# Moving the gain row's product and the second queries' transposes in the opening of a fused attention and feed-forward kernel

## The chip, the cores and the metric

The kernel runs on one core of one Trainium2 chip. The metric is the device time of one execution in microseconds (us), lower is better. A time "of the runs" is the median of several executions; durations of single instructions come from one profiled execution. The engines are TensorE (PE, with PEld for its weight loads), VectorE (DVE), ScalarE (ACT), GpSimd (POOL) and SyncE (SP); a trailing q, as in SPq, is an engine's instruction queue.

## What is computed

Chunked attention with 8 memory keys per head, then a feed-forward block with layer norm and residual. Cut to what matters (B=4, H=8, S=768, D=64, so tokens have 512 features; the hidden width is 2048):

```python
for c in range(nc):                       # chunks of 32 queries
    q_c = q[:, :, c_start:c_end]
    k_full = concat([mem_k, k[:, :, l_start:r_end]])   # 16 left, 8 right
    v_full = concat([mem_v, v[:, :, l_start:r_end]])
    a = softmax(scale * q_c @ k_full.T)
    out[:, :, c_start:c_end] = a @ v_full
x = out.transpose(0, 2, 1, 3).reshape(B, S, 512)
xn = (x - mean) / sqrt(var + 1e-6) * g_ln
return x + relu(xn @ w_ch1) @ w_ch2
```

## The kernel before, in words

The 3072 tokens are 24 tiles of 128. For a tile, `scores` multiplies turned keys (`KT`) and turned queries (`QT`) on TensorE and ScalarE takes the exponentials into `AT` (line 294); `values` multiplies `AT` with `V` (line 307); `norm` divides, sums and writes `xn` = (x - mean) * `g_row` on VectorE (lines 317 to 327); `turn_x` turns `xn` into `xT`. `up` (line 375) multiplies by `w_ch1` and `down` (line 392) by `w_ch2`, three tiles to a unit, eight units. From unit 0 on, a hand-written plan puts the attention steps of the next unit between the `up` and `down` steps of this one. The schedule is manual: each engine runs its instructions in the order in which the code issues them.

The change lies in the opening, before unit 0, where nothing but the order written out in lines 455 to 551 sets what runs when:

- Line 471, `stay_busy(10)`: ten products of zeros (`busy`, 128x128 by 128x512), whose results nobody reads. `stay_busy(n, p)` writes them to the PSUM buffer `p`, or to a slot of the `mm` ring. "Zero products" below are these.
- Line 472, `clear_v` with `clear_k`: memsets on VectorE. Line 473, `mem_keys`: four small products turn the memory keys (line 167), VectorE copies them to `memKT` (line 173). Line 474, `mem_cols`: VectorE spreads them into `KT` (line 177).
- Lines 513 to 522: the first turned keys, that is the transposes (line 187) of head pairs 0 and 1 of batch 0, 32 products; two zero products; the first turned queries, 32 products; then, on VectorE, four copies into `KT` (line 202), on ScalarE two into `QT` (line 210), on VectorE `keep_mem` (line 144); three zero products.
- Lines 523 to 532: the second keys (pairs 2 and 3), four zero products, the second queries, and their copies, of pair 2 on ScalarE and of pair 3 on VectorE.
- Lines 533 and 534: `g_row`, the gain row `g_one` (1x512, fp32) repeated over 128 partitions by a product with a column of ones, into `mm` buffer `banks[2]`; VectorE copies it to SBUF.
- Lines 535 to 563: scores, values and norms of tiles 0 to 2 with more zero products between them, then the first `up` steps, which need the weights `w1c`.

The buffer `spare`, where the zero products between the transposes go, is half 0 of `att` buffer 0. Each `att` buffer has two halves of 512 floats.

GpSimd issues the loads of keys, queries, values and weights through its DMA queue, in the written order. SyncE issues `memk32`, `g_one` and `memv32` (lines 459 to 461) first, and later the stores.

The softmax here doesn't subtract the row's maximum and nothing guards it: scores larger than these inputs give would overflow.

## Time and profile before

| What | Value |
|---|---|
| Median of 8 runs | 217.43 us (215.36 to 218.54) |
| The profiled execution: its own time | 218.06 us |
| The profiled execution: span of the trace | 216.3 us |
| PE busy | 209.2 us, 97% of the span |
| PEld busy | 124.1 us, 57% |
| DVE busy | 113.5 us, 52% |
| ACT busy, POOL busy | 91.3 us, 91.5 us, 42% each |
| Granted TensorE clock, mean | 0.99 |
| The two products of line 533 | 1.12 us busy |
| The copy of line 534 | 0.69 us |
| The 35 zero products in the opening | 26 into `mm`, 9 into `att` |

The profile lists busy time by engine and by line, the chain of work that ended last (followed back from the last instruction to what released each step), a timeline with the idle time before a group in brackets and what ended it, and windows with the granted clock. Starts are microseconds from the span's start. A line `start, length, engine, line, operation, output<-inputs, shape, xcount` of the timeline is a group of equal instructions.

### The profile page before, as it was taken

The page shows a single profiled execution, that of the slowest core. Times are in us where ns is not written, and L with a number is a line of the kernel's source. Part 1 is how long each engine was busy: PE and PEld are TensorE (multiplying, and loading weights), DVE is VectorE, ACT ScalarE, POOL GpSimd, SP SyncE. Part 2 cuts the span into 40 slices and gives each one's busy share as a digit, 9 for nine tenths or more (in the row PEclk, how much of TensorE's full clock was granted, in tenths as well). Part 3 has the DMA queues.
Part 4 walks back from the last instruction along what each step waited for, and adds up shares of the span by engine and source line. Part 5 has one row for each costly group of instructions (what it writes and reads, how often), then busy time and mean ns, then how long its engine had stood idle before and what let it go on. Part 6 is the DMA issues. An engine that isn't in the chain of part 4 may idle for free.

```text
span 216.3 us, 5336 instructions
## 1 busy us (share of the span) xinstructions
PE 209.2 (97%) x2173; PEld 124.1 (57%) x2173; DVE 113.5 (52%) x268; ACT 91.3 (42%) x187; POOL 91.5 (42%) x169
## 2 busy tenths in 40 slices
PE   7989999999999999999989999999999999999994
PEld 2545876457755566546644566447644665457553
DVE  4657484585747548524365349415375438534222
ACT  4354535954573666302734077203761175303200
POOL 7992244689998228810003999520112000400000
PEclk9988999999999999999999999999999999999999
DMA  5999999999999959995305999997693201230012
GB/s 81 159 128 194 204 216 185 192 206 247 139 139 171 127 155 127 113 202 144 54 2 100 122 179 158 148 186 82 175 141 109 84 3 24 77 122 0 0 52 97
DMA packets 87611, 27.26 MB, mean 126 GB/s; under 512 B 78289, under 2 KB 84081, under 8 KB 87538
## 3 DMA queue, kind: packets, MB, share of 16 engines
q0 software_dynamic: 62128, 14.38, 75.0%
q1 hardware_dynamic: 25458, 12.54, 26.3%
q8 instruction: 17, 0.28, 0.5%
q14 instruction: 8, 0.07, 0.1%
HBM read 28.84 MB, written 6.29 MB: 162 GB/s over the span
## 4 chain that ended last, share of the span: by engine, by line
PE 86%; DMA 6%; DVE 3%; issue 1%; POOL 1%; SPq 1%; ACT 1%; POOLq 0%; DVEq 0%; ACTq 0%
PE mm L392 38%; PE mm L375 33%; DMA V<-V 4%; PE att L307 4%; PE att L287 3%; DMA kraw<-in_k_dram 2%; PE att L187 2%; PE mm L364 2%; PE mm L410 2%; PE mm L187 1%; DVE xn L327 1%; DVE xs L318 1%; PE att L350 1%; ACT AT L294 1%; PE mm L533 0%
## 5 line engine op out<-in xcount | busy, mean ns | idle before, releaser
L375 PE MATMUL mm<-xT,w1c 128*128 128x384 f16 (+2 forms) x528 | 87.9, 322 | 0.1
L392 PE MATMUL mm<-w2c,rT 128*128 128x512 f16 x368 | 84.2, 379 | 0.0
L375 PEld LDWEIGHTS <-w1c 128*128 128x128 f16 x528 | 57.9, 114 | 24.8 <-issue 0.6
L381 ACT ACTIVATE rT<-mm 128x384 f16<-128x384 f32 (+2 forms) x66 | 31.7, 484 | 76.2 <-PE mm L375 54.8
L392 PEld LDWEIGHTS <-rT 128*128 128x128 f16 x368 | 34.4, 98 | 38.4
L383 DVE TENSOR_SCALAR rT<-mm 128x384 f16<-128x384 f32 (+2 forms) x66 | 35.6, 542 | 33.7 <-PE mm L375 33.3
L399 DVE SCALAR_TENSOR_TENSOR osb<-mm,rstd,xs 128x512 f32<-128x512 f32 x23 | 17.3, 751 | 42.4 <-PE mm L392 31.1
L294 ACT ACTIVATE AT<-att,band 104x512 f16<-104x512 f32 x48 | 29.5, 688 | 11.8 <-PE att L287 11.8
L336 POOL TENSOR_SCALAR veps<-squares 128x1 f32<-128x1 f32 x24 | 5.1, 214 | 54.3 <-ACT junk L333 53.0
L116 POOL DMA_DIRECT2D V<-in_v_dram x24 | 18.4, 773 | 12.2 <-DMA w1c<-in_moe_w_ch_dram 9.0
L333 ACT ACTIVATE junk<-xs,nmean 128x512 f16<-128x512 f32 x24 | 17.4, 724 | 7.7 <-DVE nmean L324 6.9
L327 DVE SCALAR_TENSOR_TENSOR xn<-xs,nmean,g_row 128x512 f16<-128x512 f32 x24 | 18.0, 752 | 0.9
L318 DVE SCALAR_TENSOR_TENSOR xs<-att,rec 128x512 f32<-128x512 f32 x24 | 16.6, 691 | 0.8
L274 POOL COPY KT<-KT 128x128 f16<-128x128 f16 (+4 forms) x16 | 4.3, 294 | 23.9 <-DMA KT<-kraw 23.9
L340 POOL TENSOR_TENSOR rstd<-veps,mhalf 128x1 f32<-128x1 f32 x24 | 13.2, 551 | 2.0
L307 PEld LDWEIGHTS <-AT 104*64 104x64 f16 x384 | 7.7, 112 | 8.5 <-issue 3.4
L122 POOL DMA_DIRECT2D V<-in_v_dram x16 | 12.0, 798 | 0.1
L247 POOL DMA_DIRECT2D qraw<-in_q_dram x12 | 11.4, 946 | 0.0
L247 POOL DMA_DIRECT2D kraw<-in_k_dram x12 | 11.3, 942 | 0.0
L307 PE MATMUL att<-V,AT 104*64 104x65 f16 x384 | 9.7, 199 | 1.6 <-DMA V<-V 0.9
L317 DVE RECIPROCAL rec<-att 128x8 f32<-128x8 f32 x24 | 4.9, 203 | 11.7 <-ACT AT L294 6.0
L364 PE MATMUL mm<-busy 128*128 128x512 f16 x26 | 9.2, 490 | 1.2 <-DVE counts L456 1.2
(76 smaller groups left out, 118.2 us busy)
## 6 DMA issues: line engine op xcount, KB each, us to landing
out_dram<-osb SPq DMA_DIRECT2D x23, 256.0 KB, 2.4
V<-in_v_dram POOLq DMA_DIRECT2D x36, 96.0 KB, 6.2
w1c<-in_moe_w_ch_dram POOLq DMA_DIRECT2D x4, 512.0 KB, 10.9
w2c<-in_moe_w_ch_dram POOLq DMA_DIRECT2D x4, 512.0 KB, 14.5
kraw<-in_k_dram POOLq DMA_DIRECT2D x12, 128.0 KB, 5.6
qraw<-in_q_dram POOLq DMA_DIRECT2D x12, 128.0 KB, 5.7
qraw<-in_q_dram POOLq DMA_DIRECT2D x3, 384.0 KB, 12.2
kraw<-in_k_dram POOLq DMA_DIRECT2D x3, 256.0 KB, 4.9
```

The source lines that it names most:

```text
L116: nc.gpsimd.dma_start(out=V[b % 2][r : r + hi - lo, g, :, 0:64], in_=dram(v, b * H * HS + lo * D, [[64, hi - lo], [HS, H], [1, 64]]),)
L247: nc.gpsimd.dma_start(out=free(dst, 512 * t, [[64, H], [1, 64]]), in_=dram(src, b * H * HS + 128 * t * D, [[D, 128], [HS, H], [1, 64]]),)
L294: nc.scalar.activation(out=free(a, 32 * c, [[512, 2], [64, 8], [1, 32]], KR), in_=free(p, 32 * c, [[512, 2], [64, 8], [1, 32]], KR), func= ...
L307: nc.tensor.matmul(out=p[64 * gg : 64 * gg + 64, h // 4, c0 : c0 + 65], lhsT=AT[t % 3][0:KR, h % 2, 4 * gg + h // 2, :], rhs=V[b % 2][0:KR ...
L318: nc.vector.scalar_tensor_tensor(out=x.rearrange("p (h d) -> p h d", h=H), in0=free(p, 0, [[128, H], [1, 64]]), scalar=1.0, in1=free(r, 0, ...
L327: nc.vector.scalar_tensor_tensor(out=xn[i], in0=x, scalar=nmean[i], in1=g_row, op0=ALU.add, op1=ALU.mult,)
L333: nc.scalar.activation(out=junk, in_=xs[xi], func=ACTF.Square, bias=nmean[i], accum_out=squares[i],)
L375: nc.tensor.matmul(out=p, lhsT=free(w, i, [[4, 128]]), rhs=xT[u % 2][:, dt, lo:hi], start=(dt == 0), stop=(dt == 3),)
L381: nc.scalar.activation(out=o, in_=p, func=ACTF.Relu)
L383: nc.vector.tensor_scalar(out=o, in0=p, scalar1=0.0, scalar2=None, op0=ALU.max)
L392: nc.tensor.matmul(out=p, lhsT=rT[hc][:, 128 * i : 128 * i + 128], rhs=w2c[hc // 4][:, hc % 4, :], start=(hc == 0), stop=(hc == 15),)
L399: nc.vector.scalar_tensor_tensor(out=o, in0=p, scalar=rstd[t % 9], in1=xs[t % 9], op0=ALU.mult, op1=ALU.add,)
```

## The change

The product for `g_row` and its copy move from behind the second queries to the front. The product stands behind the ten zero products and ahead of `mem_keys`; its output is now half 1 of `att` buffer 0, whose half 0 is the `spare` of the zero products. The copy stands behind `mem_cols` and so ahead of the copies of the first turned keys. Behind the second keys two zero products are left of four, then come the second queries, and three zero products stand where the product for `g_row` was.

```diff
     stay_busy(10)
     clear_v(0, nc.vector, lambda: clear_k(0), 33)
+    spare = att[(turn["att"] + 2) % 2]
+    nc.tensor.matmul(out=spare[:, 1, :], lhsT=ones32, rhs=g_one, start=True, stop=True)
     mem_keys()
     mem_cols(0)
+    nc.vector.tensor_copy(out=g_row, in_=spare[:, 1, :])
     for g in range(3):
         load_v_group(0, g)
...
     stay_busy(3, spare)
     for j in range(2, 4):
         turn_kq(first_k[j], k16[0], j, CUT[0])
-    stay_busy(4, spare)
+    stay_busy(2, spare)
     for j in range(2, 4):
         turn_kq(first_q[j], q16[0], j, CUT[1])
...
     for j in range(2, 4):
         keep_q(on[j], first_q[j], 0, j, CUT[1], 0, 6)
-    nc.tensor.matmul(out=banks[2], lhsT=ones32, rhs=g_one, start=True, stop=True)
-    vec(out=g_row, in_=banks[2])
+    stay_busy(3, spare)
     scores(0, 0)
     scores(0, 1)
     stay_busy(2)
```

## The prediction, made before the changed kernel ran

> **What bounds the kernel now.** I read the page first: PE is busy 209.2 of 216.3 us, and the chain of waits gives PE 86%. So whatever delays PE in the opening delays the end, unless something later absorbs it. The change touches only the opening, so the next view is that chain in order of time (start, length, what):

> ```profile
> 3.66 4.88 DMA kraw<-in_k_dram
> 8.53 0.04 issue
> 8.58 0.69 PE mm L187 x32
> 9.27 0.97 PE att L364 x4
> 10.24 0.61 PE mm L187 x32
> 10.85 1.05 PE mm L533 x2
> 11.90 0.36 PE att L287 x16
> ```

> Up to 8.53 a load sets the pace: the second keys can't be turned before it lands. From there to the first scores PE itself is the chain: second keys, four zero products, second queries, product for `g_row`. The timeline of VectorE shows what the copies do beside it (start, length, line, shape, idle time before):

> ```profile
> 5.11 0.29 DVE L173 CAST memKT<-mm 128x128 f16<-128x128 f32 x1 [1.56 <-PE mm L167]
> 5.44 0.26 DVE L177 COPY KT<-memKT 128x384 f16<-128x384 f16 x1
> 5.96 1.60 DVE L202 COPY KT<-mm 128x72 f16<-128x72 f16 x4 [0.27 <-PE mm L187]
> ...
> 7.59 0.96 DVE L144 COPY V<-memv 8x3072 f16<-8x3072 f16 x1
> ...
> 9.31 0.85 DVE L202 COPY KT<-mm 128x72 f16<-128x72 f16 x2 [0.76 <-PE mm L187]
> ...
> 10.89 0.56 DVE L210 COPY QT<-mm 128x384 f16<-128x384 f16 x1 [0.73 <-PE mm L187]
> ```

> VectorE has about 0.8 us of slack twice. The windows (busy time of PE, PEld, DVE, ACT, POOL, then granted clock, DMA share, GB/s) show one more thing: a stretch at half clock behind the scores.

> ```profile
> 4.00:7.40 3.40, 2.95 (x75) 1.65 (x74) 1.99 (x6) 0.21 (x1) 3.36 (x8) 1.00 1.17 185
> 7.40:10.80 3.40, 3.01 (x75) 1.66 (x72) 1.97 (x4) 1.74 (x5) 3.24 (x10) 1.00 1.70 150
> 10.80:14.20 3.40, 2.75 (x57) 1.35 (x54) 1.25 (x2) 2.17 (x5) 3.40 (x5) 1.00 1.55 100
> 14.20:17.60 3.40, 3.40 (x38) 1.55 (x37) 3.17 (x10) 1.60 (x3) 2.67 (x5) 0.50 1.17 177
> ```

> Last, how far an earlier PE could get. GpSimd's timeline:

> ```profile
> 20.13 0.80 POOL L116 DMA_DIRECT2D V<-in_v_dram  x1 [3.26 <-DMA w1c<-in_moe_w_ch_dram]
> ```

> GpSimd was held until the first `w1c` landed, and PE's first weight load from `w1c` starts at 20.09. The first `up` products start at 20.50. The same view shows it held for the second, third and fourth `w1c` until 22.63, 25.18 and 28.25. So the opening can gain at most about 20.50 - 20.09 = 0.4 us; a loss passes through in full, since PE has no idle time behind it to give.

> **Part 1: the product for `g_row` ahead of the memory keys.** It costs PE the same 1.05 us, at 4.82 instead of 10.85. Its input is there: `memv32`, issued after `g_one` on SP's queue, landed by 3.60. (No other queue is passed: no DMA moves, and GpSimd's and SP's orders are the same.) So `mem_keys` starts at 4.82 + 1.05 = 5.87, and lasts 0.25 us, to 6.12. The first keys started at 5.48 when their load landed; now they start at 6.12 and, at 0.62 us (5.48 to 6.10), end at 6.74.

> **Part 2: the copy, and the wait it brings.** On VectorE `memKT` follows `mem_keys` by 5.11 - 4.82 = 0.29: 6.16. `mem_cols` starts 0.33 later, 6.49; the copy after 0.26 + 0.03, at 6.78, and lasts 0.69, to 7.47. The diff doesn't say that somebody waits for this, but the changed program as built does: the first zero product behind the first keys writes the same `att` buffer as the product for `g_row`, and waits for VectorE; the last thing VectorE was given before it is that copy. In the old program it waits for nobody. PE is free at 6.74 and gets on at about 7.52 (a release takes 0.04 to 0.06 us, as from the exponentials' end at 13.62 to the values at 13.66). Queued behind it on PE is everything: two zero products (0.97/4 = 0.243 each, 0.49), first queries (0.62), three zero products (0.73): 7.52 + 1.84 = 9.36. That takes the place of the wait for the load until 8.53, so the second keys start 9.36 - 8.58 = 0.78 us later.

> **Part 3: behind the second keys.** Two zero products fewer ahead of the second queries: -0.49. Three zero products (0.73) instead of the product (1.05): -0.32. From 9.36: keys 0.69, two zero products 0.49, queries 0.61, three zero products 0.73, so the scores are due at 11.88, against 11.90. The sum on PE is 0.78 - 0.49 - 0.32 = -0.03 us.

> **Part 4: are the copies in time?** VectorE: the four copies of line 202 start behind the new copy at 7.50 and end at 9.10, `keep_mem` 9.13 to 10.09, the copy of pair 3's keys (0.73 behind the start of their turning, 9.36) 10.12 to 10.97. Its queries are turned from 9.36 + 0.69 + 0.49 = 10.54, the copy follows by 0.65 (10.24 to 10.89): 11.19 to 11.75. ScalarE's last copy: 10.54 + 0.40 = 10.94 to 11.42. Both end before 11.88, VectorE's with 0.13 us to spare; three zero products are its cover. If that is gone, the scores of pair 3 wait for it, by what it is late. The copy of `g_row` that leaves 11.94 ran while VectorE had nothing else, so it gives nothing.

> **Part 5: the clock.** Half clock from 14.2 to 17.6 costs in the chain 1.30 us for three zero products at 14.10, and the same at 16.52, against 0.65 for three at 18.04; 16 value products take 0.58 at 15.40 against 0.37 at 18.69. Without it, the second values would wait for the exponentials (end 14.77) and start at 14.82 instead of 15.40, and after both triples `up` could start some 1.5 us earlier, but `w1c` allows 0.4. The stretch before the half clock held 2.75 us of busy PE, with the product for `g_row`, 48 small products and one idle gap of 0.65; the stretches at 4.0 and 7.4 held 2.95 and 3.01 and were not followed by half clock. The change moves that product into 4.0 to 7.4, where the new wait also puts an idle gap of 0.63 (6.74 to 7.37); 10.8 to 14.2 gets zero products instead. No row tells what the gate counts, so I bound it: neither stretch at half clock, -0.4; half clock only moved ahead, to 7.4: zero products at 0.43 (1.30/3) and transposes at 0.58/0.37 of their time put the scores 1.33 later, but then the full clock behind 14.2 gives that back, `up` at 20.26, -0.2; both stretches, `up` at 21.15, +0.65. I take "as before", 0, between them.

> The row first: half clock came after a gap of only 0.65 us. [...]

> One more bound: the ten zero products were 0.43 us apart up to 3.78 and about 0.22 from then on. Where that step comes later in an execution, the product for `g_row` and the first keys run slow as well: up to 1.05 + 0.35 = +1.4 us. The other end is the -0.4.

> **Sum.** -0.03 on PE, 0 from copies, 0 from the clock: 218.06 - 0.03 = 218.03 us for the profiled execution. That execution is 0.63 us above the median of the runs (217.43), so for the median 217.4 us: no change.

> **Rivals.**
> - *The clock gate takes the new opening worse* (slower). Place: 7.4 to 10.8, with the product for `g_row` and the 0.63 us wait in the stretch before, and 14.2 to 17.6 still at half. For it: the stretch that was punished had the same product and the same size of gap. Against: 0.86 us of zero products at its start. Price +0.65 us, with the slow opening up to +1.4: 218.1 to 218.8. It decides if both stretches are granted 0.50. Chance 0.25.
> - *The clock stays full* (faster). For it: the product leaves 10.8 to 14.2 for zero products. Price -0.4, capped by `w1c`: 217.0. Chance 0.20.
> - *The new wait doesn't bite*, for example since the copy runs earlier. Then the second keys start at 8.58 as before and PE is due at the scores at 8.58 + 2.52 = 11.10, but VectorE (four copies to 9.1, and the rest as in part 4 without a gap: 10.09, 10.95, 11.53) holds pair 3's scores until 11.58: -0.3, 217.1. Against it: the built program has the wait. Chance 0.08.
> - *No change*, as forecast, the remaining 0.47.

> **Numbers.** 1% is 2.2 us, about what a measurement of this kernel can tell from no change. No case reaches that: not the gains, because of `w1c`, and not the losses, unless several meet. The runs themselves spread from 215.36 to 218.54. For the range I put some 0.8 us of that beside the ends -0.4 and +1.0 (middle of the slow rival): 216.2 to 219.2. Faster by over 1%: 0.05, for scatter; slower by over 1%: 0.09, the slow rival with a second loss; within 1%: 0.86.

> **What would show it.** Right: the first zero product behind the first keys waits on VectorE's copy until about 7.5; second keys at about 9.4, no longer released by a load; scores at about 11.9; first `up` between 20.1 and 21.2. Wrong: second keys at 8.6 (no wait), scores held by VectorE's last copy, half clock in a stretch other than 14.2 to 17.6, or any difference behind 21 us that isn't carried over from the opening.

## The result, and the profile after

| | before | after |
|---|---|---|
| Median of the runs | 217.47 us (32 runs, 215.26 to 219.18) | 220.5 us (11 runs, 219.48 to 221.42) |
| Ratio to before | | 1.0169, 95% interval 1.0136 to 1.0202 |
| Profiled execution: time, span | 218.06, 216.3 us | 220.38, 218.7 us |
| Mean granted clock of the profiled execution | 0.99 | 0.977 |
| First scores start, first `up` starts | 11.90, 20.50 us | 15.34, 23.46 us |

The change costs 3.0 us by the medians of all runs; forecast was none, and the range ended at 219.2. Ratios and their intervals leave out executions that lie more than 1.5% above the fastest of the same kernel (so 1.0169 is more than 220.5/217.47); where this hides part of a kernel's executions, the text gives those too.

The chain of waits of the changed kernel (start, length, what), from the first zero products to the first scores:

```profile
1.24 4.42 PE mm L364 x10
5.66 1.05 PE att L474 x2
6.71 0.20 PE mm L167 x4
...
7.52 0.61 DVE g_row L477
8.13 0.04 issue
8.17 0.59 PE att L364 x2
8.77 0.85 PE att L187 x23
9.61 1.40 PE att L364 x3
11.01 0.99 PE mm L187 x17
12.00 0.97 PE att L364 x2
12.97 0.98 PE mm L187 x17
13.95 1.40 PE att L364 x3
15.34 0.96 PE att L287 x24
```

PE's timeline has the wait beside the first zero product that follows the first keys:

```profile
8.17 0.59 PE L364 MATMUL att<-busy 128*128 128x512 f16 x2 [0.66 <-DVE g_row L477]
```

So the wait for the copy is there, with the order that was foreseen. But three zero products take 1.40 us where the sum had 0.73, and the second keys 0.99 instead of 0.69. The windows say why (busy time of PE, PEld, DVE, ACT, POOL, each with its count, then granted clock, DMA share, GB/s):

```profile
5.20:8.60 3.40, 2.74 (x42) 1.20 (x40) 1.63 (x5) 0.00 (x0) 3.20 (x13) 1.00 1.23 181
...
8.80:12.00 3.20, 3.20 (x68) 1.97 (x67) 2.10 (x4) 1.24 (x4) 3.20 (x4) 0.52 2.02 132
12.00:15.40 3.40, 3.40 (x45) 1.40 (x45) 1.41 (x3) 0.82 (x2) 3.40 (x6) 0.50 1.28 117
15.40:18.70 3.30, 3.27 (x52) 1.68 (x49) 0.59 (x2) 2.42 (x4) 1.23 (x4) 0.50 1.23 200
...
18.90:19.10 0.20, 0.20 (x2) 0.00 (x0) 0.17 (x3) 0.00 (x0) 0.20 (x1) 0.50 1.30 195
19.10:19.30 0.20, 0.20 (x3) 0.06 (x4) 0.17 (x2) 0.00 (x0) 0.20 (x1) 0.86 1.16 195
```

From about 8.9 to 19.15 the clock is halved: 10.2 us, three times the 3.4 us of the one stretch in the old profile (14.2 to 17.6), while PE is busy nearly all the time. That is one execution; the mean clock stands beside every one. "A halved stretch", below, is 3.4 us of half clock, as in the old profile. Half clock over 10.2 of 218.7 us makes a mean of 1 - 10.2 x 0.5 / 218.7 = 0.977; by the same sum one stretch of 3.4 makes 0.992 and two make 0.984. Of 12 executions of the changed kernel (the eleven of the table and one of 220.11 us) 11 have 0.974 to 0.977. Of 67 of the old one, run beside the experiments, 40 have 0.997 or more (median 216.9 us), 19 have 0.990 to 0.992 (217.3), 7 have 0.983 or 0.984 (218.3), one has 0.975 (221.3). So the time goes with the number of halved stretches that the mean stands for, in the old kernel too, and the change moves nearly all executions to three. The longer start of the changed profile (its ten zero products take 4.42 us against 3.64) is not what brings the half clock: below, they take 4.45 us in a run whose opening shows none, and 3.86 us in one with four halved stretches.

At the first `up` the changed kernel is 23.46 - 20.50 = 2.96 us late, at the end 2.4. Part comes back at one place: the old kernel's values of unit 2 waited 0.9 us for the transfer `V<-V`, until 109.96; in the changed kernel no product waits for it, though one waits 0.2 us for VectorE's `rT`. So the prediction's "PE has no idle time behind it to give" was not quite right.

### The profile page after: what moved, and what is told of

Its sections match the earlier page's. It is cut to its first block, busy times and chain, and to the rows that moved or that the text cites. A ratio compares the mean times of both kernels' runs of the same rounds, so it can differ in the third digit from the quotient of the medians.

```text
span 218.7 us, 5338 instructions
## 1 busy us (share of the span) xinstructions
PE 212.8 (97%) x2174; PEld 125.6 (57%) x2174; DVE 113.4 (52%) x268; ACT 91.2 (42%) x187; POOL 91.5 (42%) x169
## 4 chain that ended last, share of the span: by engine, by line
PE 95%; DVE 3%; issue 0%; DVEq 0%
PE mm L375 37%; PE mm L392 37%; PE mm L364 4%; PE att L307 4%; PE att L287 3%; PE att L187 2%; PE att L364 2%; PE mm L410 2%; PE mm L187 2%; DVE xn L327 1%; DVE xs L318 1%; PE att L350 1%; PE att L474 0%; DVE rT L383 0%; DVE KT L177 0%
## 5 line engine op out<-in xcount | busy, mean ns | idle before, releaser
L116 POOL DMA_DIRECT2D V<-in_v_dram x24 | 18.9, 792 | 10.4 <-DMA w1c<-in_moe_w_ch_dram 7.7
L122 POOL DMA_DIRECT2D V<-in_v_dram x16 | 12.0, 796 | 0.1
L317 DVE RECIPROCAL rec<-att 128x8 f32<-128x8 f32 x24 | 4.9, 203 | 12.3 <-PE att L307 7.5
L364 PE MATMUL mm<-busy 128*128 128x512 f16 x26 | 9.9, 522 | 1.2 <-DVE counts L456 1.2
L287 PEld LDWEIGHTS <-KT 64*128 64x128 f16 x384 | 6.8, 97 | 6.0 <-issue 5.9
```

The lines of the kernel that those rows point to most:

```text
L116: nc.gpsimd.dma_start(out=V[b % 2][r : r + hi - lo, g, :, 0:64], in_=dram(v, b * H * HS + lo * D, [[64, hi - lo], [HS, H], [1, 64]]),)
L364: nc.tensor.matmul(out=p, lhsT=busy[:, 0:128], rhs=busy, start=True, stop=True)
```

## The experiments

The edits are against the changed kernel, unless said otherwise. All ratios are to the kernel before, on the same chip.

**The wait away.** The product goes where no zero product writes:

```diff
-    spare = att[(turn["att"] + 2) % 2]
-    nc.tensor.matmul(out=spare[:, 1, :], lhsT=ones32, rhs=g_one, start=True, stop=True)
+    nc.tensor.matmul(out=mm[1], lhsT=ones32, rhs=g_one, start=True, stop=True)
...
-    nc.vector.tensor_copy(out=g_row, in_=spare[:, 1, :])
+    nc.vector.tensor_copy(out=g_row, in_=mm[1])
```

> The changed kernel with the product for g_row written to buffer 1 of the mm ring, which the zero products between the transposes don't use; so no zero product waits for the copy. Theory A (the clock gate: the 3.4 us stretch that holds the product and the 0.66 us wait has too few dense products, and the gate halves the clock for three stretches; the wait is the larger part): half clock at most one stretch, mean clock 0.99, ratio to before 0.997 to 1.005, first up at about 20.5. Theory B (the product itself, one row of fp32 for 1.05 us, is what starves the gate; the wait hardly matters): half clock still from about 9, clock 0.977, ratio 1.010 to 1.017, first up at 22.8 to 23.4. Theory C (fewer zero products behind the second keys): as B.

Ratio 0.9963 (0.9921 to 1.0004). Median of all ten executions 217.08 us; three of them, at 218.63, 218.87 and 222.7, stand outside the ratio. In the profiled execution (215.79 us) the first `up` starts at 19.52, and with the product in front but no wait the clock stays at 1.00:

```profile
5.20:8.60 3.40, 3.40 (x58) 1.61 (x58) 1.29 (x5) 0.00 (x0) 3.20 (x13) 1.00 1.25 182
8.80:12.00 3.20, 3.20 (x86) 1.80 (x80) 3.14 (x7) 2.06 (x5) 3.20 (x4) 1.00 2.06 133
```

The long half clock is gone as a rule: theory A, not B or C. Two details speak for the product too: with it in front, the clock record still has two halved stretches in two of ten, and the execution of 222.7 us, with a recorded clock of 1.0, is of the kind that the last section describes.

**The front alone.** Rear as before, product and copy in front:

```diff
-    stay_busy(2, spare)
+    stay_busy(4, spare)
     for j in range(2, 4):
         turn_kq(first_q[j], q16[0], j, CUT[1])
...
-    stay_busy(3, spare)
     scores(0, 0)
```

> Only the front of the change: product and copy ahead of the memory keys and first keys; behind the second keys four zero products as before, and nothing where the product was (so five zero products fewer on that path than four plus the product, by time). Theories A and B: half clock from about 9 as in the changed kernel, clock 0.977, ratio 1.012 to 1.02. Theory C (the two zero products that are missing behind the second keys): no long half clock, ratio below 1.005. A sum of path lengths alone would give 9.36 + 0.69 + 0.97 + 0.61 = 11.63 for the scores, 0.27 us earlier than before.

Ratio 1.018 (1.0105 to 1.0255), clock 0.967 in the profiled execution, half clock from 7.8 to 21.5, four stretches:

```profile
8.00:21.40 13.40, 13.11 (x192) 6.68 (x191) 6.52 (x16) 5.12 (x11) 9.48 (x15) 0.50 1.42 159
```

The front does the harm without the rear; theory C falls.

**The rear alone** (against the kernel before):

```diff
-    stay_busy(4, spare)
+    stay_busy(2, spare)
...
     vec(out=g_row, in_=banks[2])
+    stay_busy(3, spare)
```

> Only the rear of the change: two zero products instead of four behind the second keys, the product for g_row and its copy where they were, and the three zero products behind them. Theories A and B: no half clock before 14, at most one stretch, clock 0.99 or more; by path the scores come 0.73 - 0.49 = 0.24 us later, ratio 1.000 to 1.003. Theory C: half clock from 9 to 12 on, ratio above 1.01.

Ratio 0.9983 (0.9948 to 1.0017); one of ten executions had clock 0.974 and 221.81 us, the others lie from 216.17 to 217.51. The profiled one has a single halved stretch, but from 11.1 and for 3.4 us, not behind 14 as expected: it again follows the stretch with the product for `g_row`, which runs from 10.1 to 11.1 here. The rear costs nothing that could be measured.

**Zero products in place of the product, the wait kept:**

```diff
-    nc.tensor.matmul(out=spare[:, 1, :], lhsT=ones32, rhs=g_one, start=True, stop=True)
+    stay_busy(5, spare[:, 1, :])
```

> The changed kernel with five zero products (5 x 0.216 = 1.08 us) in place of the product for g_row, into the same half of the same buffer; the copy and the wait for it stay. g_row is then all zeros, so the layer norm's output, and with it the feed-forward part, is left at zero; the instructions and their order are otherwise the same. Theory A: the wait is still there, so still half clock for part of the opening, ratio 1.006 to 1.017. Theory B: the gate has its dense products, clock 0.99 or more, ratio 0.997 to 1.005 in spite of the wait.

Ratio 0.9973 (0.9938 to 1.0007), all ten executions from 215.76 to 217.87, clock never under 0.997. This is the run that breaks theory A as stated, for the wait is there in full. The timeline of PE (line numbers one higher than in the changed kernel):

```profile
5.21 1.24 PE L365 MATMUL att<-busy 128*128 128x512 f16 x5
6.38 0.25 PE L168 MATMUL mm<-identity,memk 128*64 128x64 f16 x4
6.56 0.69 PE L188 MATMUL mm<-identity,kraw 64*64 64x64 f16 x32
7.91 0.59 PE L365 MATMUL att<-busy 128*128 128x512 f16 x2 [0.66 <-DVE g_row L478]
```

The idle time is the same 0.66 us, to the hundredth, as in the changed kernel, and so is the busy time of PE from 5.2 to 8.6:

```profile
5.20:8.60 3.40, 2.74 (x54) 1.47 (x54) 1.89 (x6) 0.00 (x0) 3.18 (x13) 1.00 1.22 177
8.80:12.00 3.20, 3.20 (x92) 1.91 (x86) 2.69 (x5) 2.06 (x5) 3.20 (x4) 1.00 1.91 128
```

**The wait covered.** Three more zero products that wait for nothing, ahead of the two that do:

```diff
+    stay_busy(3, first[:, 0, :])
     stay_busy(2, spare)
     for j in range(2):
         turn_kq(first_q[j], q16[0], j, CUT[1])
```

> The changed kernel with three zero products more, into a buffer that nothing holds (half 0 of att buffer 1), ahead of the two that wait for the copy: the 0.66 us wait is filled, the wait itself and the order of all else stay. Theory D (what decides is how much dense product the 3.4 us stretch holds; product for g_row and idle time are both thin, and either may be replaced): no run of half clock over three stretches, mean clock mostly 0.99 to 1.0, ratio 0.996 to 1.005. Theory E (the wait delays the copies, and this, not the idle time of TensorE, is what the changed kernel pays for): still 1.010 to 1.017.

Ratio 0.9997 (0.9954 to 1.0041). Eight of ten executions from 215.77 to 217.96, and two at 221.75 and 222.63, outside the ratio, of which below. Theory D; E would have needed 1.010 or more. Work was added to PE, and the ratio went from 1.0169 to 0.9997. The execution that was profiled is the one of 222.63 us, so that the filled wait is shown by the times and the recorded clocks of the eight (0.997 or more), not by a trace.

**More zero products where the clock is already halved:**

```diff
     keep_mem(0, 0, 6, vec)
-    stay_busy(3, spare)
+    stay_busy(6, spare)
```

> The changed kernel with six zero products instead of three behind the first queries, where the clock is already halved. Theory D (a stretch at half clock ends when the next one holds enough dense product, and the transposes count for little): the first halved stretch has 6 x 0.43 = 2.6 us of dense product and is the last or last but one, mean clock 0.984 to 0.992 in place of 0.977, ratio 1.004 to 1.012, faster than the changed kernel although it does more work. If busy time alone counted, nothing would change in the clock and the ratio would be about 1.02 or above.

Half right. Two of four executions have clock 0.984 (the others 0.976 and 0.998), and the profiled one is halved from 7.7 to 14.5, two stretches:

```profile
7.80:11.00 3.20, 3.15 (x37) 1.47 (x37) 2.46 (x5) 0.86 (x2) 3.04 (x7) 0.50 1.97 158
11.00:14.40 3.40, 3.40 (x38) 1.36 (x36) 0.84 (x2) 0.72 (x2) 3.40 (x6) 0.50 1.38 95
14.80:18.00 3.20, 2.55 (x75) 1.40 (x69) 0.56 (x1) 2.15 (x4) 1.95 (x4) 1.00 1.21 191
```

The six did not fall into the first stretch, as expected, but half into each (9.84 to 12.51). The ratio is 1.0167 (1.01 to 1.0234), that of the changed kernel (1.0169): at half clock the added three cost 2.67 - 1.40 = 1.27 us, which probably ate what the shorter half clock saved. Neither expected ratio (1.004 to 1.012, or about 1.02 and above) was met, though the interval of four executions touches both.

**What makes the product thin: fp32 or one row?** Five products of fp16, one row each:

```diff
+    nc.scalar.copy(out=g16, in_=g_one)
...
-    nc.tensor.matmul(out=spare[:, 1, :], lhsT=ones32, rhs=g_one, start=True, stop=True)
+    for _ in range(5):
+        nc.tensor.matmul(out=spare[:, 1, :], lhsT=ones16, rhs=g16, start=True, stop=True)
```

> The changed kernel with five fp16 products of one row (1x128 ones by the 1x512 gain row rounded to fp16, each into the same place, 5 x 0.216 = 1.08 us) in place of the fp32 product; g_row is then rounded to fp16; order, copy and wait as in the changed kernel. If one row in use is what makes the product thin: half clock as in the changed kernel, clock 0.977, ratio 1.010 to 1.017. If fp32 is what makes it thin: full clock as with zero products of 128 rows, clock 0.99 or more, ratio 0.996 to 1.004.

Ratio 1.0181 (1.0109 to 1.0253), four executions from 219.47 to 222.01, two of them with clock 0.974 and 0.977. Against the run with five zero products of 128 rows (0.9973) the type and the 512 columns are the same, and the rows differ, with them the data. So it is not fp32: with five fp16 products of zeros in 128 rows the recorded clock was 0.997 or more in all ten executions, and with five of ones and gains in one row 0.974 and 0.977 in two of four, with 221.42 and 222.01 us in the two that recorded 0.998 and 1.0. That the one row does it, and not the data, is my guess; no run separates them.

**Zero products missing, nothing else** (against the kernel before):

```diff
-    stay_busy(10)
+    stay_busy(6)
```

> The kernel before with six zero products at its start in place of ten; product for g_row and its copy where they were, no new wait. By path lengths nothing changes: TensorE then waits for the first keys' load until 5.48 as before. Theory D (dense product missing from the first stretches is enough, whoever takes its place): the clock is released late or halved early, for three stretches or more, ratio 1.010 to 1.025. If the product at the front or the wait for its copy matters by itself: ratio 0.998 to 1.003.

A mixed answer. Five of ten executions lie from 215.0 to 217.78, the other five from 219.81 to 222.66; the median of all is 218.79 against 216.97 (the ratio, 0.9991, holds only the first five). So four zero products fewer cost as much, without the moved product and without a wait for a copy, but only in some executions, where I had expected it in all. It is not the same loss in detail: four of the five long executions have a recorded clock of 0.991 to 1.0, not 0.977. And PE is idle for longer too, 1.30 us before the first keys where it was 0.41. In the profiled execution (217.53 us) zero products are slow until about 12 us, though every window says 1.00 (chain, start, length, what):

```profile
8.54 1.40 PE att L364 x3
9.94 0.99 PE mm L187 x17
10.93 1.40 PE att L364 x4
12.33 0.61 PE mm L187 x32
```

**A version meant to beat both.** The gain row in two fp16 parts that are added in PSUM, so 0.43 us of one-row products (2 x 0.216; five zero products take 1.08 with the zeros in front), in the gap where PE waits for the first keys, copied by ScalarE; the rear as in the change:

```diff
+    nc.scalar.copy(out=g_hi, in_=g_one)
...
-    spare = att[(turn["att"] + 2) % 2]
-    nc.tensor.matmul(out=spare[:, 1, :], lhsT=ones32, rhs=g_one, start=True, stop=True)
+    nc.vector.tensor_tensor(out=g_lo, in0=g_one, in1=g_hi, op=ALU.subtract)
     mem_keys()
     mem_cols(0)
-    nc.vector.tensor_copy(out=g_row, in_=spare[:, 1, :])
+    for i, part in enumerate((g_hi, g_lo)):
+        nc.tensor.matmul(out=mm[1], lhsT=ones16, rhs=part, start=(i == 0), stop=(i == 1))
+    nc.scalar.copy(out=g_row, in_=mm[1])
```

> A version meant to beat both: the gain row split into two fp16 parts (VectorE and ScalarE, while idle), two one-row fp16 products (0.43 us in place of 1.05) behind the memory keys, where TensorE waits 0.41 us for the first keys, into buffer 1 of the mm ring, copied on ScalarE, which is idle from 4.2 to 7.4; the rear as in the change. Second keys at 8.6 as before, scores at 8.6 + 2.52 = 11.1 in place of 11.9, up held by w1c until about 20.1. Theory D: mostly full clock, ratio 0.993 to 0.998. If earlier scores bring more idle time and with it half clock behind 14: 0.998 to 1.003.

> The version with two fp16 parts once more, with more rounds: ratio 0.995 to 1.000, mean clock 0.997 or more in nearly all executions, while the kernel before has a halved stretch in about half of its own. up is held by w1c, so nothing below 0.995.

Ratios 0.9979 (0.9942 to 1.0017) and 1.0001 (0.9966 to 1.0037): no gain on the kernel before that could be measured, though the recorded clock was 0.997 or more in all 22 executions (three of them, at 219.27 to 219.94 us, stand outside the ratios; the last section comes back to them). Its scores came at 11.43 in the profiled execution, not 11.1, because the ten zero products ended 0.8 us later than in the old profile. And then the weights held it, as the sum had them:

```profile
19.65 0.52 PE L377 MATMUL mm<-xT,w1c 128*128 128x256 f16 x3 [0.99 <-DMA w1c<-in_moe_w_ch_dram]
```

PE sat idle for 0.99 us until `w1c` landed. A faster opening ends there.

## Why the prediction was wrong, point by point

**The product in front** cost 1.05 us, as summed (5.66 to 6.71). It started 0.84 us later, because the ten zero products ran at 0.43 us apart to their end (4.42 us against 3.64). This was the bound "where that step comes later in an execution"; it was priced, and left out of the likeliest case on the strength of one profile.

**The wait for the copy** was foreseen and right in kind and size: from the start of the first keys to the first zero product behind them 1.35 us (6.82 to 8.17) against 1.40 (6.12 to 7.52), copy 0.68 against 0.69. The idle time was 0.66 us; the prediction gave 0.63 in one part and 6.74 to 7.52, which is 0.78, in another.

**The rear** was right as a sum of lengths: from the second keys to the scores 2.52 us were due, and at full clock the run with the other buffer took 2.53 (9.70 to 12.23), as did the one with zeros in front (9.80 to 12.33). In the changed kernel itself it took 4.3 at half clock. The -0.03 us came from setting this against the later start of the second keys.

**The copies in time** were right in that they didn't hold the scores; PE got there at 15.34, VectorE's last copy ended at 14.55. In the two runs at full clock the scores wait for no copy either. With the front alone, where no three zero products cover the copy, they wait 0.27 us for it.

**The clock is the step that failed.** The sentence is: "I take 'as before', 0, between them." The place and mechanism stood in the slow rival (the product and the wait in one stretch, and half clock behind it), with chance 0.25 and a price of +0.65 us, or up to +1.4 with a slow start; the two were not added. Measured: +3.0 us. The likeness that spoke for the rival held: the old stretch from 10.8, with the product, a gap of 0.65 us and 2.75 us of busy PE, was followed by half clock, and so was the new one, with the product, a gap of 0.66 and 2.74. What was wrong in every bound was the length: half clock was given one stretch at a place, 7.4 to 10.8 or 14.2 to 17.6, and "then the full clock behind 14.2 gives that back", with no reason why it should end after one. In the run it went on for three in a row. One of the prediction's own signs of being wrong, half clock in a stretch other than 14.2 to 17.6, came true; a loss of over 1% had a chance of 0.09.

The loss can be followed in the prediction's own sum. The scores were due at 11.88 and came at 15.34, 3.46 us later. PE got on behind the wait at 8.17 instead of 7.52: 0.65 us, what was left of the slow start's 0.84. From there to the scores it took 7.17 us instead of 4.36: 2.81 us, at half clock. In the run with the other buffer the same work takes 4.43 us (7.86 to 12.29) at full clock.

Why it went on for three stretches is in part open. The busy column doesn't tell: PE was busy 3.20 of 3.20 and 3.40 of 3.40 us. By the chain, the second halved stretch (about 12.3 to 15.7) held some 2.0 us of zero products, 1.0 of transposes and 0.4 of scores, and half clock went on; the third (to 19.15) held about 2.2 us of zero products, and more scores, and values, where the second had transposes, and the clock came back. That suggests that transposes count for little, as does the run with six zero products, where half clock ended one stretch earlier in two of four executions; it doesn't show it.

**The cap on gains** by `w1c` is there, as the two-part version shows, but its size, 0.4 us, came from one execution: there the first `up` starts at 19.65, and in the run with the other buffer at 19.52, some 0.9 us before the old 20.50, and the times of the runs still show no gain that could be measured.

**Gaps and lengths.** The longest gap in the stretch before the halving was 0.66 us. Half clock lasted 3.4 us in the profiled executions of the old kernel and of the rear alone, 6.8 with six zero products behind the first queries, 10.2 in the changed kernel and 13.7 with the front alone, where the bounds had 3.4 at a place. Ten equal zero products took 3.64 (old kernel), 3.86 (front alone), 4.12 (zeros in front) or 4.45 us (other buffer).

What stays open: what exactly the granted clock follows. With the product and the wait it was 0.50 behind them; with the product and no wait (the other buffer) 1.00 in the profiled opening; with 128-row zero products in place of the product, and the wait kept, it was 1.00 (0.997 or more in all ten executions), and with zero products in the wait, and the product kept, 0.997 or more in the eight executions up to 217.96 us. That the transposes count for little is a guess from the lengths above; no run isolates them. How many zero products it takes could not be read, because the stretches fall differently: half clock began at 7.7, 7.8, 8.9, 11.1 and 14.2 in the five profiled executions that show it.

## What to carry to other kernels

Where zero products are there for the clock, as here (with six of the first ten, five of ten executions took 219.81 us or more), ask of a move what it takes their place with: here a one-row product of 1.05 us and a wait of 0.66 us came among them, and the price was not the 0.7 us of the wait but 3 us by way of half clock (0.50 for 10.2 us). Before a product is moved, look for the buffer that it shares with what follows: here the output in the other half of the zero products' buffer made the wait, and another buffer (0.9963) or three zero products as cover (0.9997) removed the loss in most executions; one of ten and two of ten still took 221.75 us or more. Before a clock term is set to "as before", look at the granted clock and the time of every execution, not of one profile, and ask what would end a half clock once it has begun.

## What the runs showed that was not expected

A recorded mean clock of 1.00 went with products as slow as at 0.50. The profiled execution of the run with five one-row fp16 products has a span of 220.3 us and a mean clock of 1.0, and no window of its opening shows less. But its zero products are as slow as under half clock until after 20 us. Timeline of PE (zero products stand in line 366 here):

```profile
4.64 1.06 PE L366 MATMUL mm<-busy 128*128 128x512 f16 x2
5.63 2.31 PE L479 MATMUL att<-g,ones 1*128 1x512 f16 x5
...
15.72 1.46 PE L366 MATMUL att<-busy 128*128 128x512 f16 x3
...
21.67 0.60 PE L366 MATMUL mm<-busy 128*128 128x512 f16 x2
```

Three zero products take 1.46 us at 15.72, the length they have in the changed kernel at 13.88 under a recorded 0.50; at 21.67 two take 0.60. My guess, which no row shows, is that the clock was low from the start of the execution without a record of it, and that the ten zero products (4.45 us here) did not bring it up. In the old profile too the first zero products are 0.43 us apart, up to 3.78, and 0.22 from then on, both under a recorded 1.00.

Three executions of this kind were profiled: this one, the one of 222.63 us with the wait covered, and, with slow products until about 12 us only, that of six zero products at the start (217.53 us). More of them are probably behind the times of 220.6 us and over with a clock of 0.998 to 1.0: one each of the changed kernel (221.37), the other buffer (222.7), the front alone (221.32) and the six behind the first queries (220.63), two with the wait covered (221.75, 222.63), two of this run (222.01, 221.42) and three with six at the start (222.22, 221.17, 220.77). The old kernel has none in 67 executions (the longest with 0.997 or more took 218.28 us), nor have the rear alone and the zeros in front in ten each; with 0.43 us of one-row products in front, the two-part version has three of 22, of 219.27 to 219.94 us. So a one-row product directly behind the ten zero products seems to carry a second risk, which taking the wait away does not remove (222.7 us with the other buffer). The reading to trust is the distance between equal products, as 0.43 against 0.22 us in the opening of the old profile.
